# The opening joins the build-time order, and the inverses' triangle is split over two PSUM banks by rows

## The chip, the cores and the metric

The kernel runs on one core of a Trainium2 chip. The metric is device time in microseconds (us) of one execution. Three executions of the kernel before took 611.55, 602.25 and 604.9 us, median 604.9; the profiled execution, from which every row below comes, took 604.67 us.

## The reference

Two stages. The first is a recurrent attention over 4 batches, 8 heads, 768 time steps and a head dimension of 40, with a 40x40 state per batch and head:

```
y[t]  = r[t] . S
Sa    = S . a[t]
S     = S * w[t] - outer(Sa, b[t]) + outer(v[t], k[t])
```

The second treats y, laid out as 3072 tokens of 320 values, as the input of a mixture of 8 experts. A token is computed where x . w_skip > 0; its expert is the argmax of x . w_gate, and the output is x + gate * (relu(x W1) W2), with W1 320x1024 and W2 1024x320. Other tokens pass unchanged.

## The kernel before

**The tiling.** The 768 steps are cut into 24 chunks of 32 steps (c = 0 to 23) and 12 half-phases of 64 (h = 0 to 11); six phases ph hold two half-phases or four chunks each. The 32 pairs of batch and head are spread over partitions and columns, so that one small matmul serves one pair.

**Per half-phase.** The inputs w, k and b, and a are loaded (`load_w`, `load_kb`, `load_a`). VectorE runs two scans (`scan_z`, `scan_w`) that turn the decays into cumulative products, with a clamp and a reciprocal between them (`scan_d`). `kbm` and `l1a` multiply k, b and a by these products, on POOL or VectorE. `wchk` lets ScalarE square w with a running sum, for a range check. `m1` forms the 32x32 products inside a chunk on TensorE; ScalarE copies one half of them into AB, VectorE transposes the other half, which is masked (`fin`) and sent by four DMAs into the left operand L1. `kbt` and `wtt` transpose operands on TensorE.

**Per phase.** The recurrence inside a chunk needs the inverse of a triangular 32x32 matrix for each pair. `tinv` does this on VectorE for phases 1 to 5: a forward substitution with, in each step, a product and a subtraction of the rest of the triangle. The triangle lies in PSUM in two pieces by columns, the first SPL = 12 columns in X0 (32x12 values in each partition) and the other 20 in X1 (20x20). The steps of the two pieces are independent; step i of the loop does step i of X0 and step i+12 of X1, each with a product and a subtraction: 30 products and 30 subtractions for X0, 18 and 18 for X1, 96 in all. ScalarE copies the result to SBUF and a VectorE transpose of 128x1024 puts it in TB. `tinv0` does phase 0 in another way: two 16x16 blocks of the triangle on VectorE in SBUF, the rest by matmuls (`s1`, `s2`, `full`).

**Per chunk.** `ux`, `uq`, `sst` and `yy` are the recurrence, 32 to 64 small matmuls each, for x = 0 and 1. `ux` needs the chunk's R, `uq` multiplies its result by TB, four copies put that into R, a masking on POOL follows, `sst` makes the state for the next chunk's R, `yy` the output Y, which goes out as XS, one DMA per chunk. The router of the experts (`score4`, `route`) runs two chunks behind.

**What sets the order.** Two regimes follow one another. From the first load to the end of chunk 0's pass through the loop, the order is the order of the program's text, written out by hand: the opening. It issues each instruction as it is met (line 117, in `Rec.call`). From c = 1 the recorder is on (`if c==1: rec.on=True`): every call becomes a task with the data that it reads and writes, a cost and a latency, and at c = 22 `flush` orders all tasks of chunks 1 to 21 by a list scheduler at build time (`plan`) and issues them (line 233). The plan starts with every engine free at time 0 and all data from before already there. It knows costs per operation (`cost`), gives each task that uses PSUM a bank, lets VectorE take a ScalarE copy out of PSUM, and counts a DMA as landed a fixed 2.2 us plus its bytes over 170 GB/s after its issue. From c = 22 the text's order holds again (line 117), for the last two chunks and the experts.

**The opening's order.** Half-phases 0 and 1 are loaded and scanned; h = 2 is loaded, and its scans stand ahead of the inverse of phase 0; h = 3 and its scans, `kbm` and `l1a` come between the pieces of `s1` and `s2`. For h = 3 both `kbm` and the first `l1a` are given to VectorE (`kbm(3,1,V); kbm(3,0,V); l1a(3,0,V)`), the second `l1a` to POOL. Chunk 0's second half (`uq(0,1)`) is the first piece of chunk 1's recorded work. Between the steps stand bursts: `zb` and `warm` issue 128x512 matmuls whose result nobody reads (`burst`; BU0 = 6 at the start, the counts of BX after it).

Of the kernel before, what the change touches and what calls it, by code (L numbers as in the profile page):

```python
# [8 lines left out]
F32 = mybir.dt.float32  # L9
# [47 lines left out]
class Rec:  # L57
# [58 lines left out]
    def call(s,e,op,fn,a,k):  # L116
        if not s.on: return fn(*a,**k)  # L117
        def ap(x):
            if x is None or isinstance(x,(int,float,str)): return []
            if hasattr(x,'tensor'): return [x]  # L120
            return ap(x.ap) if hasattr(x,'ap') else []
        w=ap(a[0])+ap(k.get('accum_out'))
        r=[y for x in list(a[1:])+[v for n,v in k.items() if n!='accum_out'] for y in ap(x)]
        W=[u for x in w for u in s.use(x)]; R=[u for x in r for u in s.use(x)]
        d,lat=s.cost(e,op,w,r,a)
        own=dict(s.own)
        L=s.tasks[-1] if s.tasks else None
# [24 lines left out]
    def plan(s,keep=False):  # L152
# [14 lines left out]
        def want(i):  # L167
# [8 lines left out]
                a,k=max(x for x in av if x[0]<=a)  # L176
                got[o]=k; t0=max(t0,a)
            return t0,got
        pos=blk=0; ent=0.0
        done=0; old=sorted(users)  # L180
        while done<N:
            best=None
# [19 lines left out]
            if e=='P':  # L202
                pos+=t.k
                while pos>=256*(blk+1):
                    x=max(fin[i],ent+s.BLK); fin[i]=x; ent=x; blk+=1
            free[e]=fin[i]; [pool[f].remove(i) for f in pool if i in pool[f]]; done+=1; nxt[e]+=1
            for j in t.n:
                rdy[j]=max(rdy[j],fin[i]+t.lat+(s.HOP if e!=T[j].e or t.lat else 0)); left[j]-=1
                if not left[j]: put(j)
            for o in t.al:  # L210
                use.setdefault(o,{})[e]=fin[i]; users[o]-=1; last[o]=max(last.get(o,0),fin[i]+s.HOP)
# [38 lines left out]
class Ring:  # L250
# [4 lines left out]
    def tile(s,shape,dt,tag=None,name=None):  # L255
# [4 lines left out]
        if len(shape)==2: return t  # L260
        ax=["abcd"[q] for q in range(len(shape)-1)]
        return t.rearrange("p ("+" ".join(ax)+") -> p "+" ".join(ax),**{a:v for a,v in zip(ax,shape[1:])})
G2=1; TD=(1,3); BU0=6; BU=(2,0,0,0); BX=(0,0,0,0,0,1,0,0,0,0,2,2,1,1,1,0,0,0,1,2,0,1,1,1,1,0,1,0,0); SPL=12; SCAN_POOL=0; RN=192; RB=((),()); RLAST=(('0c','1b','3a','3c'),('0a','0c')); P2=0
ROUTE=('0c',('0c','1b','3c'),('0c','1b','3c'))
WT=(1,0,0,0,1)
def attn(ctx,tc,i,m,out):
# [174 lines left out]
    def tinv(ph):  # L441
        ab=AB[0]
        NLt=sq(NL_)
        V.transpose(NLt.rearrange("p a b -> p (a b)"),ab.rearrange("p a b -> p (a b)"))
        Xi=sq(X_); K=32-SPL
        X0=ps_x.tile([128,32,SPL],F32); X1=ps_x.tile([128,K,K],F32)
        V.tensor_tensor(X0,NLt[:,0:SPL].rearrange("p s t -> p t s"),m.mT[:,:,0:SPL],ALU.mult)
        V.tensor_tensor(X1,NLt[:,SPL:32,SPL:32].rearrange("p s t -> p t s"),m.mT[:,SPL:32,SPL:32],ALU.mult)
        V.memset(X0.rearrange("p a b -> p (a b)")[:,0:SPL*SPL:SPL+1],-1.0)
        V.memset(X1.rearrange("p a b -> p (a b)")[:,::K+1],-1.0)  # L450
        yield
        for i in range(1,31):
            q=[]
            for g,(j,o,X) in enumerate(((i,0,X0),(i+SPL,SPL,X1))):
                if j>30: continue
                n=31-j; k=min(i,SPL) if g==0 else i
                tv=tmp_[g][:,:n*k].rearrange("p (a b) -> p a b",b=k)
                V.tensor_tensor(tv,NLt[:,j,j+1:32].unsqueeze(2).broadcast_to([128,n,k]),X[:,j-o,0:k].unsqueeze(1).broadcast_to([128,n,k]),ALU.mult)
                q.append((tv,X[:,j+1-o:32-o,0:k]))
            for tv,xv in q: V.tensor_tensor(xv,xv,tv,ALU.subtract)  # L460
            yield
        A.copy(Xi[:,:,0:SPL],X0); A.copy(Xi[:,SPL:32,SPL:32],X1)
# [114 lines left out]
    def yy(c,x):  # L577
# [8 lines left out]
        if x==1:  # L586
# [2 lines left out]
            V.tensor_tensor(xs.rearrange("p (h e) -> p h e",h=8),Y,H[c//2]['WT',cc].rearrange("p h x e -> p (h x) e"),ALU.mult)  # L589
            SP.dma_start(ov[c],xs)  # L590
    def burst(k,l,r):
        pb=ps_s.tile([128,r.shape[1]],F32)
        for _ in range(k): TE.matmul(pb,l,r,start=True,stop=True)
    def warm(k): burst(k,m.tri,m.mc[:,0:512])
    def run_all(g):
        for _ in g: pass
    if 1:

        with tc.manual_schedule(engines={ET.Pool}):
# [9 lines left out]
            G.memset(WR[:,8192:10240],0.0)  # L609
            zero(WR[:,10240:11264])  # L610
            V.memset(l3,0.0)
            load_w(0); load_kb(0); load_a(0); load_w(1,alt[:,0:1041]); load_kb(1); load_a(1,a1)
            m.consts()
            zb=lambda n,q=0: burst(n,zl[:,128*q:128*q+128],z[:,0:512])
            zb(BU0)
            wchk(0,0); wchk(0,1)
# [3 lines left out]
            scan_z(0,None,V); scan_d(0); scan_w(0,V); load_w(2)  # L620
# [6 lines left out]
            ev=[]; late=[]; pq=ps_p; ps_p=Ring.of(ps_p.t+ps_c.t+ps_y.t+ps_x.t)  # L627
            for x in range(2):
                for c in range(2): m1(0,x,c,ev,None,V)
                warm(BX[14+x])  # L630
            for x in range(2):
                for e in ev[2*x:2*x+2]: e()
                l1a(1,x,V)
            load_a(2,L1t[:,3072:4096].rearrange("p (u t) -> p u t",u=16));
            for b in range(4): kbt(0,b); warm(BX[16+b])
            wchk(1,0); wchk(1,1)
            del ev[:]
            scan_z(2,None,V); scan_d(2); scan_w(2,V)
            kbm(2,1); kbm(2,0); l1a(2,0); l1a(2,1)
            for x in range(2):  # L640
                for c in range(2): m1(1,x,c,ev,late)
            for x in range(2): m2(0,x); warm(BX[20+x])
            for e in ev: e()
# [3 lines left out]
            t0=tinv0(Xi); next(t0); tq=[0]  # L647
            def Tb(k,n=0):
                for _ in range(k): next(t0)
                if n: q=tq[0]; tq[0]+=1; V.memset(zl[:,128*q+127:128*q+128],0.0); zb(n,q)  # L650
            ps_p=Ring.of(pq.t+ps_y.t+ps_x.t)
            ux(0,0); wex(0,0); warm(BX[24]); ux(0,1); wtt(0,0); wex(0,1)
            warm(BX[22]); wtt(0,1); warm(BX[23])
            for e in late: e()
            scan_x(1)
            wchk(2,0); wchk(2,1)
            load_w(4); load_kb(4)
            G.memset(L1t[:,2048:3072],0.0)
            ev=[]
            m2(1,0); Tb(4,BX[0]); m2(1,1); Tb(3,BX[1])  # L660
            m1(2,0,0,ev); m1(2,0,1,ev)
            Tb(2,BX[2]); Tb(2,BX[3])
            m1(2,1,0,ev); m1(2,1,1,ev)
            Tb(3,BX[4]); s1,s2,full=next(t0)
            r4=ps_p; ps_p=ps_c
            s1(0,0); warm(BX[5])
            full(0)
            s2(0,0,(0,1,0,1))
            warm(BX[11])
            uq(0,0)  # L670
            for e in ev: e()
            ps_p=r4
            zero(L1t[:,3072:4096])
            scan_z(3,alt[:,1041:2083],V); scan_d(3); scan_w(3,V); kbm(3,1,V); kbm(3,0,V); l1a(3,0,V)
            l1a(3,1); scan_x(2); scan_x(3)
            s1(0,1); warm(BX[6])
            s1(1,0)
            sst(0,0); warm(BX[12])
            s2(0,1,(1,1,1,1))
            s1(1,1); warm(BX[13])  # L680
            load_a(4)
            wchk(3,0); wchk(3,1)
            warm(BX[10])
            ps_p=pq
# [18 lines left out]
            return xl,m.route(xl[:,0:1],1,NC-2,lambda: onehot(0)),onehot  # L703
        for c in range(NC):
            ph,j=divmod(c,4)
            if c==1: rec.on=True
            if c==20: m.load(0)
            if c==22:
                with tc.manual_schedule(engines={ET.Pool}): rec.flush()
# [451 lines left out]
```

## Time and profile before

| | |
|---|---|
| profiled execution | 604.67 us |
| its span, first to last instruction | 602.5 us |
| median of three executions | 604.9 us |
| PE busy | 477.5 us, 79% |
| DVE (VectorE) busy | 463.2 us, 77% |
| ACT (ScalarE) busy | 359.3 us, 60% |
| POOL (GpSimd) busy | 305.3 us, 51% |
| DMA | 82.03 MB, mean 136 GB/s |
| mean granted TensorE clock | 0.908 of full speed |

Busy time counts the overlap of two instructions of an engine once. A line of the profile names a line of the kernel: L117 is whatever was issued in the text's order, L233 whatever the plan ordered. Tiles of the work memory M appear as M whatever their use; px, pc, pq, py and ps are PSUM banks.

### The profile page before, as it was taken

Reading aid. Unit: us, or ns where it says so; the run is one execution under the profiler, and the core shown is the slowest. Engines: PE = TensorE matmul, PEld = TensorE weight load, DVE = VectorE, ACT = ScalarE, POOL = GpSimd, SP = SyncE. Lnnn points to the kernel's source line nnn. Section 1 sums busy time; section 2 is a strip of 40 time slices with the busy share of each in tenths; the row PEclk is TensorE's granted clock in tenths of the full one; section 3 lists DMA queues with packets and bytes.
Section 4 is the critical chain, followed back from the end, with each engine's and each line's share of the span. In section 5 each row is a group of like instructions: output and inputs, shape, how many; then the busy total and the mean of one; then the engine's idle time right before and its main releaser. Section 6 shows DMA issues by size and latency. Waiting matters only on the chain. (4 is left out here: it accounts for less than half of the span.)

```text
span 602.5 us, 28644 instructions
## 1 busy us (share of the span) xinstructions
PE 477.5 (79%) x12452; PEld 397.2 (66%) x12452; DVE 463.2 (77%) x1100; ACT 359.3 (60%) x846; POOL 305.3 (51%) x225
## 2 busy tenths in 40 slices
PE   4784826897878777887798768887478999999995
PEld 1452525776666566666686556665365799999994
DVE  8988948798998699798978879872373558788871
ACT  6462636677768478667666566866265555455530
POOL 5462684465614695257755452403112266666671
PEclk9686968899799899999869979999588999999998
DMA  7874078435452635555543674453652487786100
GB/s 196 216 185 114 20 184 226 106 95 151 112 148 76 156 94 137 132 129 153 124 106 109 165 173 103 112 128 76 167 160 81 126 221 224 226 230 200 41 21 23
DMA packets 80694, 82.03 MB, mean 136 GB/s; under 512 B 49041, under 2 KB 68062, under 8 KB 80099
## 3 DMA queue, kind: packets, MB, share of 16 engines
q1 hardware_dynamic: 78643, 76.35, 48.6%
q0 software_dynamic: 1920, 3.79, 1.8%
q8 instruction: 100, 1.64, 1.2%
q14 instruction: 31, 0.25, 0.1%
HBM read 62.69 MB, written 13.15 MB: 126 GB/s over the span
## 5 line engine op out<-in xcount | busy, mean ns | idle before, releaser
L233 POOL TENSOR_TENSOR R1t<-R1t,mc 64x512 f32<-64x512 f32 x42 | 60.9, 1450 | 90.8 <-ACT R1t L233 51.5
L233 ACT COPY R1t<-pc 32x288 f32<-32x288 f32 (+4 forms) x121 | 52.7, 437 | 20.7 <-PE pc L233 12.5
L117 POOL TENSOR_TENSOR WL<-WR,WH 128x1280 fp32r<-128x1280 f32 (+1 forms) x21 | 58.0, 2798 | 8.4 <-ACT WH L117 8.3
L233 ACT COPY R1t<-px 32x288 f32<-32x288 f32 (+4 forms) x91 | 40.3, 443 | 16.0 <-PE px L233 6.1
L233 POOL TENSOR_TENSOR WR<-WR,M 104x1024 f32<-104x1024 f32 x14 | 32.4, 2334 | 15.1 <-DVE M L233 10.3
L117 ACT CAST WH<-WR 128x1024 fp32r<-128x1024 f32 (+1 forms) x35 | 39.7, 1134 | 0.0
L117 POOL DMA_INDIRECT out<-ro,ti x16 | 15.7, 984 | 45.1 <-DVE ro L117 11.1
L233 DVE TENSOR_TENSOR_SCAN M<-M 104x1041 f32<-104x1041 f32 (+1 forms) x14 | 37.7, 2695 | 0.1
L117 ACT ACTIVATE hH<-pc 128x512 fp32r<-128x512 f32 x21 | 12.6, 599 | 37.9 <-PE pc L117 31.7
L117 DVE TENSOR_TENSOR WL<-WR,WH 128x1024 fp32r<-128x1024 f32 (+1 forms) x19 | 23.8, 1254 | 12.5 <-ACT WH L117 11.9
L117 DVE CAST ti<-xe 128x2 int32<-128x2 f32 x8 | 33.1, 4132 | 0.2
L233 POOL DMA_INDIRECT xg<-XS,ix x18 | 18.4, 1022 | 28.1 <-DVE XS L233 16.8
L117 PE MATMUL pc<-xH,WH 128*128 128x256 f32 x126 | 32.5, 283 | 0.0
L233 POOL TENSOR_TENSOR M<-M,mc 128x256 f32<-128x256 f32 x18 | 18.0, 998 | 26.4 <-DVE M L233 14.8
L233 ACT COPY R1t<-py 32x416 f32<-32x416 f32 (+4 forms) x56 | 25.3, 451 | 8.0 <-PE py L233 4.6
L117 PE MATMUL ps<-WH,hH 128*128 128x320 f32 x88 | 27.6, 314 | 0.0
L117 PE MATMUL pc<-xH,WL 128*128 128x256 f32 x126 | 27.3, 281 | 0.0
L117 PE MATMUL ps<-WL,hH 128*128 128x320 f32 x88 | 27.2, 309 | 0.0
L117 PE MATMUL ps<-WH,hL 128*128 128x320 f32 x88 | 27.2, 309 | 0.0
L233 DVE TENSOR_TENSOR pc<-pc,M 128x48 f32<-128x48 f32 (+20 forms) x96 | 25.8, 269 | 1.8
L117 ACT COPY R1t<-pc 32x416 f32<-32x416 f32 (+3 forms) x36 | 15.6, 440 | 18.0 <-DVE R1t L117 11.6
L117 PE MATMUL ps<-mc 128*128 128x512 f32 x34 | 22.8, 778 | 4.4 <-DMA mc<-mc 2.9
(478 smaller groups left out, 1653.6 us busy)
## 6 DMA issues: line engine op xcount, KB each, us to landing
WR<-w SPq DMA_DIRECT2D x16, 640.0 KB
WR<-w SPq DMA_DIRECT2D x16, 512.0 KB
L2t<-SCR SPq DMA_DIRECT2D x40, 160.0 KB
WR<-kb SPq DMA_DIRECT2D x32, 160.0 KB
WR<-w SPq DMA_DIRECT2D x16, 256.0 KB
R1t<-vt SPq DMA_DIRECT2D x48, 80.0 KB
SV<-vv SPq DMA_DIRECT2D x48, 80.0 KB
out<-XS SPq DMA_DIRECT2D x24, 160.0 KB
```

The costliest lines, as they stand in the source:

```text
L117: if not s.on: return fn(*a,**k)
L233: for fn,a,k,own in s.tasks[i].calls: (fn if s.en[i]==s.tasks[i].e else s.nc.vector.tensor_copy)(*[at(x,own) for x in a],**{n:at(x,own) fo ...
```

## The change

**The order.** `rec.on=True` moves from c = 1 to just before the first load. The opening becomes tasks of the same plan as chunks 1 to 21; memsets ahead of it stay as they are. `burst` returns at once while the recorder is on, so that the bursts of the opening and of chunk 1 are gone; those after the flush (WT, two bursts of two records) remain. The opening's text is rewritten: h = 0 and 1, the inverse of phase 0 with `s1`, `full`, `s2`, then `uq(0,0)`, and only then the loads and scans of h = 2 and 3. `kbm(3,1)`, `kbm(3,0)` and `l1a(3,0)` lose their V and so go to POOL, their default. The plan's data dependencies, not this text, decide what may run when; the text sets the tasks' numbers, which enter their priority.

**The plan's DMA.** A DMA issued by SP now passes through one queue: it begins at the later of the queue's end and its issue plus 1.6 us, adds its bytes over 200 GB/s to the queue's end, and lands 0.4 us later. This holds for every DMA of the plan.

**The inverse.** The triangle is cut by rows: X0 holds rows 0 to 15 (16x16), X1 rows 16 to 31 (16x32). Step j has one product of (31-j) x j values for all rows below, and a subtraction for each bank that has such rows: two for j below 15, one from there on. So 30 products and 44 subtractions, 74 in all, on the same number of values. `tinv0` is unchanged.

```
 class Task:
-    __slots__=(...,"v")
+    __slots__=(...,"v","by")
...
+        t.by=4*int(np.prod([d[1] for d in w[0].ap])) if 'dma' in op else 0
...
-        pos=blk=0; ent=0.0
+        pos=blk=0; ent=dq=0.0
...
+            lat=t.lat
+            if e=='S': dq=max(dq,fin[i]+1.6)+t.by/2e5; lat=dq+0.4-fin[i]
             for j in t.n:
-                rdy[j]=max(rdy[j],fin[i]+t.lat+(s.HOP if e!=T[j].e or t.lat else 0)); left[j]-=1
+                rdy[j]=max(rdy[j],fin[i]+lat+(s.HOP if e!=T[j].e or t.lat else 0)); left[j]-=1
...
-        X0=ps_x.tile([128,32,SPL],F32); X1=ps_x.tile([128,K,K],F32)
+        X0=ps_x.tile([128,16,16],F32); X1=ps_x.tile([128,16,32],F32)
...
-        for i in range(1,31):
-            q=[]
-            for g,(j,o,X) in enumerate(((i,0,X0),(i+SPL,SPL,X1))):
-                if j>30: continue
-                n=31-j; k=min(i,SPL) if g==0 else i
-                tv=tmp_[g][:,:n*k].rearrange("p (a b) -> p a b",b=k)
-                V.tensor_tensor(tv,NLt[:,j,j+1:32].unsqueeze(2).broadcast_to([128,n,k]),X[:,j-o,0:k].unsqueeze(1).broadcast_to([128,n,k]),ALU.mult)
-                q.append((tv,X[:,j+1-o:32-o,0:k]))
-            for tv,xv in q: V.tensor_tensor(xv,xv,tv,ALU.subtract)
+        for j in range(1,31):
+            n=31-j; d=max(0,15-j)
+            tv=tmp_[j%2][:,:n*j].rearrange("p (a b) -> p a b",b=j)
+            V.tensor_tensor(tv,NLt[:,j,j+1:32].unsqueeze(2).broadcast_to([128,n,j]),(X0[:,j] if j<16 else X1[:,j-16])[:,0:j].unsqueeze(1).broadcast_to([128,n,j]),ALU.mult)
+            if d: V.tensor_tensor(X0[:,j+1:16,0:j],X0[:,j+1:16,0:j],tv[:,0:d],ALU.subtract)
+            V.tensor_tensor(X1[:,16-n+d:16,0:j],X1[:,16-n+d:16,0:j],tv[:,d:n],ALU.subtract)
             yield
...
     def burst(k,l,r):
+        if rec.on: return
...
+            rec.on=True
             load_w(0); load_kb(0); load_a(0); load_w(1,alt[:,0:1041]); load_kb(1); load_a(1,a1)
             m.consts()
...
+            t0=tinv0(Xi)
+            for _ in range(15): next(t0)
+            s1,s2,full=next(t0)
+            ux(0,0); wex(0,0); ux(0,1); wtt(0,0); wex(0,1); wtt(0,1)
+            scan_x(1)
+            for w in range(2): s1(0,w)
+            full(0)
+            for w in range(2): s2(0,w,(0,1,0,1))
+            m2(1,0); m2(1,1)
+            uq(0,0)
+            load_w(2); load_a(2,L1t[:,3072:4096].rearrange("p (u t) -> p u t",u=16))
+            scan_z(2,None,V); scan_d(2); scan_w(2,V); wchk(2,0); wchk(2,1); scan_x(2)
+            kbm(2,1); kbm(2,0); l1a(2,0); l1a(2,1)
...
+            scan_z(3,alt[:,1041:2083],V); scan_d(3); scan_w(3,V); wchk(3,0); wchk(3,1); scan_x(3)
+            kbm(3,1); kbm(3,0); l1a(3,0); l1a(3,1)
             load_w(4); load_kb(4)
...
-            if c==1: rec.on=True
```

## Rows read from the trace of the kernel before

**Rows 1.** The view that cuts the span into stretches: for each stretch its length, then each engine's busy us (and instructions), the granted TensorE clock, the DMA engines' busy share and GB/s. The first stretch is the opening, the others the planned chunks up to the end of the last inverse.

```profile
0.00:86.00 86.00, 50.33 (x1186) 29.59 (x1186) 70.51 (x91) 40.81 (x101) 49.39 (x43) 0.80 0.60 150
86.00:143.00 57.00, 46.32 (x1667) 38.64 (x1668) 47.13 (x143) 40.65 (x111) 29.22 (x21) 0.88 0.61 151
143.00:208.00 65.00, 51.62 (x1744) 41.67 (x1742) 59.37 (x165) 45.97 (x116) 33.93 (x25) 0.90 0.48 127
208.00:278.00 70.00, 56.67 (x2110) 46.71 (x2114) 60.32 (x174) 50.19 (x131) 44.88 (x36) 0.97 0.48 125
278.00:343.00 65.00, 53.67 (x1782) 43.77 (x1772) 55.01 (x162) 44.79 (x114) 36.90 (x31) 0.89 0.46 123
343.00:409.00 66.00, 51.84 (x1768) 42.02 (x1769) 54.11 (x185) 45.43 (x116) 21.43 (x21) 0.95 0.53 130
```

**Rows 2.** The timeline at the end of the last inverse: start us, us, engine, line, operation, tiles and shape, count, and in brackets the engine's idle time before it and what ended that.

```profile
406.94 1.94 DVE L233 STREAM_TRANSPOSE TB<-M 128x1024 f32<-128x1024 f32 x1
...
408.94 0.92 PE L233 MATMUL pc<-UX,TB 32*32 32x104 f32 x32 [0.24 <-DVE XS L233]
```

**Rows 3.** The timeline where the text's order hands over to the plan, by engine: ScalarE, SP, TensorE, VectorE.

```profile
84.96 0.72 ACT L233 ACTIVATE junk<-M,wc 104x512 bf16<-104x512 f32 x1 [10.57 <-DMA M<-wt]
...
79.65 0.85 SPq L117 DMA_DIRECT2D M<-wt  x2
...
73.61 0.92 PE L233 MATMUL px<-UX,TB 32*32 32x104 f32 x32
86.54 1.08 PE L233 MATMUL py<-WR,L1t 128*32 128x64 f32 x32 [12.02 <-issue]
...
86.12 0.32 DVE L233 STREAM_TRANSPOSE M<-py 128x128 f32<-128x128 f32 x1 [7.14 <-issue]
```

**Rows 4.** The timeline of VectorE inside the inverse of phase 2 (a subtraction of the first piece, the start of the second piece, then both pieces in turn) and at the tail of that of phase 1, where one piece is left.

```profile
158.87 0.32 DVE L233 TENSOR_TENSOR py<-py,M 128x150 f32<-128x150 f32 x1
159.10 1.43 DVE L233 TENSOR_TENSOR pq<-M,mc 128x400 f32<-128x400 f32 x1
...
160.87 0.32 DVE L233 TENSOR_TENSOR M<-M,py 128x168 f32<-128x168 f32 x1
161.11 0.18 DVE L233 TENSOR_TENSOR M<-M,pq 128x34 f32<-128x34 f32 x1
161.22 0.34 DVE L233 TENSOR_TENSOR py<-py,M 128x168 f32<-128x168 f32 x1
...
135.34 0.17 DVE L233 TENSOR_TENSOR M<-M,px 128x12 f32<-128x12 f32 x1
135.54 0.18 DVE L233 TENSOR_TENSOR px<-px,M 128x12 f32<-128x12 f32 x1
```

**Rows 5.** The timeline of the opening where VectorE and POOL work on SBUF at the same time: a product of VectorE beside one of POOL at 11 to 16 us, a scan alone and a scan beside POOL, and h = 3's `kbm` and first `l1a`. A time that stands for two instructions (x2) is their sum.

```profile
12.45 3.15 DVE L117 TENSOR_TENSOR WR<-M 40x1024 f32<-40x1024 f32 x1
...
11.36 3.17 POOL L117 TENSOR_TENSOR WR<-WR,M 104x1024 f32<-104x1024 f32 x1 [4.92 <-DMA WR<-kb]
...
32.22 2.33 DVE L117 TENSOR_TENSOR_SCAN M<-M 104x1041 f32<-104x1041 f32 x1 [2.37 <-DMA M<-wt]
...
35.08 3.87 DVE L117 TENSOR_TENSOR_SCAN M<-M 104x1040 f32<-104x1040 f32 x1
...
34.62 6.30 POOL L117 TENSOR_TENSOR WR<-WR,M 104x1024 f32<-104x1024 f32 x2 [9.48 <-DVE M L117]
...
65.78 3.89 DVE L117 TENSOR_TENSOR WR<-WR,L2t 104x1024 f32<-104x1024 f32 x2
...
69.59 1.74 DVE L117 TENSOR_TENSOR L1t<-SCR,M 40x1024 f32<-40x1024 f32 x1
```

**Rows 6.** The groups of POOL instructions: busy us, mean ns of one, and idle time before them. And POOL's idle time ahead of chunk 0's masking, from the timeline.

```profile
L233 POOL TENSOR_TENSOR WR<-WR,M 104x1024 f32<-104x1024 f32 x14 | 32.4, 2334 | 15.1 <-DVE M L233 10.3 <-DMA WR<-kb 4.7
L233 POOL TENSOR_TENSOR L1t<-M 40x1024 f32<-40x1024 f32 x8 | 17.5, 2182 | 2.6 <-DVE M L233 2.3
...
65.29 1.63 POOL L117 TENSOR_TENSOR R1t<-R1t,mc 64x512 f32<-64x512 f32 x1 [15.83 <-issue]
```

**Rows 7.** The bursts: one line of the view of the PSUM tile ps for each of the two kinds (count, shortest/median/longest ns of one, first and last start), and the timeline around the burst ahead of `uq(0,0)`.

```profile
L117 PE MATMUL ps<-mc x30: 592/615/1222, 20.5 to 72.1; 128*128 128x512 f32 x30
...
L117 PE MATMUL ps<-SV,SV x12: 592/592/1222, 3.1 to 10.0; 128*128 128x512 f32 x12
...
58.53 3.65 PE L117 MATMUL ps<-mc 128*128 128x512 f32 x4
62.11 0.92 PE L117 MATMUL pc<-UX,TB 32*32 32x104 f32 x32
```

**Rows 8.** The stretches again, ten microseconds each, TensorE alone: busy us (instructions), granted clock, DMA share, GB/s.

```profile
50.00:60.00 10.00, 5.78 (x157) 0.50 0.42 119
...
80.00:90.00 10.00, 3.46 (x118) 0.54 0.82 190
...
100.00:110.00 10.00, 9.84 (x270) 0.51 0.60 159
```

**Rows 9.** ScalarE's last copies of `m1`'s products into AB ahead of the inverse of phase 0 (x2 is the sum of two), and the transpose with which VectorE begins that inverse.

```profile
31.81 0.65 ACT L117 COPY M<-px 128x128 f32<-128x128 f32 x2
...
39.68 1.20 DVE L117 STREAM_TRANSPOSE M<-M 128x1024 f32<-128x1024 f32 x1
```

More of the change, by code (lines that the diff above doesn't have):

```diff
@@ L39 @@
 class Task:
-    __slots__=("e","op","calls","R","W","d","lat","out","p","n","pr","al","up","k","v")
+    __slots__=("e","op","calls","R","W","d","lat","out","p","n","pr","al","up","k","v","by")
 class Eng:
@@ L262, in tile @@
         return t.rearrange("p ("+" ".join(ax)+") -> p "+" ".join(ax),**{a:v for a,v in zip(ax,shape[1:])})
-G2=1; TD=(1,3); BU0=6; BU=(2,0,0,0); BX=(0,0,0,0,0,1,0,0,0,0,2,2,1,1,1,0,0,0,1,2,0,1,1,1,1,0,1,0,0); SPL=12; SCAN_POOL=0; RN=192; RB=((),()); RLAST=(('0c','1b','3a','3c'),('0a','0c')); P2=0
+G2=1; TD=(1,3); BU0=6; BU=(2,0,0,0); BX=(0,0,0,0,0,1,0,0,0,0,2,2,1,1,1,0,0,0,1,2,0,1,1,1,1,0,1,0,0); SCAN_POOL=0; RN=192; RB=((),()); RLAST=(('0c','1b','3a','3c'),('0a','0c')); P2=0
 ROUTE=('0c',('0c','1b','3c'),('0c','1b','3c'))
@@ L444, in tinv @@
         V.transpose(NLt.rearrange("p a b -> p (a b)"),ab.rearrange("p a b -> p (a b)"))
-        Xi=sq(X_); K=32-SPL
-        X0=ps_x.tile([128,32,SPL],F32); X1=ps_x.tile([128,K,K],F32)
[L447 to L450, printed above, removed]
-        yield
-        for i in range(1,31):
-            q=[]
-            for g,(j,o,X) in enumerate(((i,0,X0),(i+SPL,SPL,X1))):
-                if j>30: continue
-                n=31-j; k=min(i,SPL) if g==0 else i
-                tv=tmp_[g][:,:n*k].rearrange("p (a b) -> p a b",b=k)
-                V.tensor_tensor(tv,NLt[:,j,j+1:32].unsqueeze(2).broadcast_to([128,n,k]),X[:,j-o,0:k].unsqueeze(1).broadcast_to([128,n,k]),ALU.mult)
-                q.append((tv,X[:,j+1-o:32-o,0:k]))
-            for tv,xv in q: V.tensor_tensor(xv,xv,tv,ALU.subtract)
+        Xi=sq(X_)
+        X0=ps_x.tile([128,16,16],F32); X1=ps_x.tile([128,16,32],F32)
+        V.tensor_tensor(X0,NLt[:,0:16,0:16].rearrange("p s t -> p t s"),m.mT[:,0:16,0:16],ALU.mult)
+        V.tensor_tensor(X1,NLt[:,:,16:32].rearrange("p s t -> p t s"),m.mT[:,16:32],ALU.mult)
+        V.memset(X0.rearrange("p a b -> p (a b)")[:,::17],-1.0)
+        V.memset(X1.rearrange("p a b -> p (a b)")[:,16::33],-1.0)
+        yield
+        for j in range(1,31):
[4 more added lines that the diff above has]
+            V.tensor_tensor(X1[:,16-n+d:16,0:j],X1[:,16-n+d:16,0:j],tv[:,d:n],ALU.subtract)
             yield
-        A.copy(Xi[:,:,0:SPL],X0); A.copy(Xi[:,SPL:32,SPL:32],X1)
+        A.copy(Xi[:,0:16,0:16],X0); A.copy(Xi[:,16:32],X1)
         s0=(2*ph)%NTB; s1=(2*ph+1)%NTB
@@ L611, in attn @@
             V.memset(l3,0.0)
+            rec.on=True
             load_w(0); load_kb(0); load_a(0); load_w(1,alt[:,0:1041]); load_kb(1); load_a(1,a1)
             m.consts()
-            zb=lambda n,q=0: burst(n,zl[:,128*q:128*q+128],z[:,0:512])
-            zb(BU0)
-            wchk(0,0); wchk(0,1)
             for x in range(2): zero(fR(x,0))
@@ L619, in attn @@
             load_vv(0,0); load_vv(0,1); load_rr(0); load_kb(2)
-            scan_z(0,None,V); scan_d(0); scan_w(0,V); load_w(2)
+            scan_z(0,None,V); scan_d(0); scan_w(0,V)
+            wchk(0,0); wchk(0,1)
             kbm(0,1); kbm(0,0,V); l1a(0,0,V); scan_z(1,alt[:,1041:2083],V); l1a(0,1,V)
@@ L626, in attn @@
             zero(Xi.rearrange("p a b -> p (a b)"))
-            ev=[]; late=[]; pq=ps_p; ps_p=Ring.of(ps_p.t+ps_c.t+ps_y.t+ps_x.t)
             for x in range(2):
-                for c in range(2): m1(0,x,c,ev,None,V)
-                warm(BX[14+x])
+                for c in range(2): m1(0,x,c,FE=V)
+                l1a(1,x,V)
+            for b in range(4): kbt(0,b)
+            wchk(1,0); wchk(1,1)
             for x in range(2):
-                for e in ev[2*x:2*x+2]: e()
-                l1a(1,x,V)
@@ L634, in attn @@
[L634 to L643, printed above, removed]
+                for c in range(2): m1(1,x,c)
@@ L644, in attn @@
+            for x in range(2): m2(0,x)
             for x in range(2):
                 for c in range(2): SP.dma_start(L2[x][0][64*x:64*x+64,c],i['idl'][x,64*x:64*x+64])
-            load_kb(3); load_w(3,alt[:,0:1041]); load_a(3,a1)
[L647 to L656, printed above, removed]
-            load_w(4); load_kb(4)
[L658 to L680, printed above, removed]
+            t0=tinv0(Xi)
@@ L681, in attn @@
+            kbm(2,1); kbm(2,0); l1a(2,0); l1a(2,1)
+            load_kb(3); load_w(3,alt[:,0:1041]); load_a(3,a1)
+            for w in range(2): s1(1,w)
+            G.memset(L1t[:,2048:3072],0.0)
+            m1(2,0,0); m1(2,0,1); m1(2,1,0); m1(2,1,1)
+            zero(L1t[:,3072:4096])
+            scan_z(3,alt[:,1041:2083],V); scan_d(3); scan_w(3,V); wchk(3,0); wchk(3,1); scan_x(3)
+            kbm(3,1); kbm(3,0); l1a(3,0); l1a(3,1)
+            load_w(4); load_kb(4)
+            sst(0,0)
             load_a(4)
-            wchk(3,0); wchk(3,1)
@@ L683, in attn @@
-            warm(BX[10])
-            ps_p=pq
             for x in range(2):
```

## The prediction

> **What bounds the kernel now.** I read the stretches first, to see which engine sets the pace in each part, then the end of the last inverse, then the place where the two orders meet, and last the single instructions that the change touches. In the first 409 us VectorE is busy 346.5 us, the sum of its six entries, or 85%; TensorE is busy 310.5 us, 76%, ScalarE and POOL less [rows 1]. That VectorE's queue ends this part, and not the recurrence, is seen at its end: the transpose that finishes the last inverse runs from 406.94 to 408.88 us, and the matmul that needs it starts 0.06 us later [rows 2]. What follows takes the remaining 193.6 us of the span and is untouched by the change, so I take a microsecond of VectorE's queue saved before 408.9 us as a microsecond of the total, as long as nothing else becomes late.
>
> VectorE's idle time before that point is 62.6 us. 25.4 us of it lie in the first 143 us (15.5 and 9.9), the other 37.2 in the four stretches after [rows 1]. The largest single piece stands where the text's order hands over to the plan: ScalarE waits 10.57 us for a load of w that SP issued only at 79.65 us, behind it wait the copies that empty m1's bank, TensorE is idle 12.02 us and VectorE 7.14 us [rows 3]. The plan, starting with all earlier data "there", had put the range check on that load first.
>
> **The change part by part.** *The seam.* With one plan from the first load on there is no place where data under way counts as landed, and the copies need not stand behind the check. On VectorE's queue the stall is worth 7.1 us; the ends are 0 (it forms again elsewhere) and 12.0, TensorE's idle time [rows 3]. I take -7.1, since VectorE is the engine whose sum matters. If it goes, what is late next is the first full inverse, which needs h = 2 and 3 scanned.
>
> *The inverse.* Per inverse 22 of 96 instructions go, 110 in all; the values, 2 x 4960, stay. The price hangs on whether neighbours depend on each other. Independent neighbours: 168 values start 0.24 us before the next, 34 values 0.11 us, so 0.97 ns per value and 0.08 us fixed. Dependent ones: 0.20 us for 12 values, so 0.19 us fixed [rows 4]. Before, with the pieces in turn, 18 double steps cost 4 x 0.08 and 12 single ones 2 x 0.19: 10.4 us fixed. After, 14 steps cost 0.19 + 0.08 + 0.08 (the second subtraction covers the first) and 16 cost 2 x 0.19: 11.0 us. So perfect alternation before would make the change cost 0.6 us per inverse, 3 in all; if every removed instruction gave back the dependent price, it would save 4.2 per inverse, 21 in all. Between +3 and -21 I take -5, near the first end, because rows 4 show neighbours overlapping, a little below it because the plan knows nothing of that overlap and does not alternate strictly; the piece that starts late (159.10 us, after the first has done six steps) shows it [rows 4].
>
> The Trainium skill, page "VectorE: DVE Perf Modes", section "The DRAIN you can't avoid", says that the next instruction does not start until the pipe is empty, and advises to lower the count of instructions. By it the sum would take -21 here, that is 571 us; the trace disagrees, with 0.11 us between two starts where the first runs 0.18 [rows 4].
>
> *The three products that move.* kbm(3,1), kbm(3,0) and l1a(3,0) leave VectorE, 3.89 + 1.74 = 5.6 us [rows 5], for POOL, at 2 x 2.33 + 2.18 = 6.9 us [rows 6]. POOL has room, idle 15.8 us around there before [rows 6]; queued behind the three are the maskings of chunk 0 and of m1(2), which yy and L1's DMAs wait for. But POOL's products slow VectorE's: a product of 40x1024 takes 3.15 us and ends 1.1 us after POOL's, a scan takes 3.87 us beside POOL against 2.33 alone [rows 5]. If each of the three hits a neighbour for 1.5 us, 1.0 of the 5.6 is left; if none, all of it. I take -3.
>
> The Trainium skill, page "SBUF — State Buffer", section "SBUF: two separate sides", speaks against this move: a VectorE instruction with two SBUF inputs and a POOL instruction that reads SBUF exclude each other for the whole instruction. By it the move could give back up to POOL's 6.9 us and cost 1.3 on balance, 591 us in all; the 3.15 us row agrees, but the loop's steps read one operand from PSUM.
>
> *The rest of the opening's order.* The 2.37 us that VectorE waits for w(2) [rows 5] goes, as other work is there by then: -2.4, the ends 0 and -2.4. The inverse of phase 0 could start when AB is complete, at 32.46 us and not at 39.68 [rows 9]; but the scans that stand there are done later on the same queue, so 0 for the sum. On SP the loads of w(2) and a(2) pass behind four idl DMAs and L1's; DMA engines are busy 60% in the opening [rows 1], and VectorE's queue of half-phases 0 and 1 covers it. If the cover is gone, the scan of h = 2 waits again, for about those 2.4 us. POOL's later kbm(2) follows the scan as before. PSUM banks are given by the plan now; I cost that at 0, covered by TensorE's 46 idle us in the first 143.
>
> *The bursts.* 30 + 12 records go, about 18.5 + 7.1 = 26 us of TensorE at their medians; one group of 3.65 us stood directly ahead of uq(0,0) [rows 7]. TensorE doesn't bound here: 0, with a gain of 3.7 at most; the loss is a rival below.
>
> *The plan's DMA queue* alters the order of all chunks up to 21. No row shows the new order. I take 0, and as bounds a quarter of VectorE's 37.2 idle us there: -9 to +9.
>
> Sum: -7.1 - 5 - 3 - 2.4 = -17.5. The profiled execution's own time is 604.67 us, 2.2 more than its span and 0.2 below the median of the three runs, so no correction is needed: **587 us**.
>
> **The rivals.** *The stall only moves* (597 us, 592 to 605). SP issues in order, ScalarE too; a check planned on a load that lands later than counted blocks the copies again, somewhere in the first 100 us where DMA is 60% busy. Then the seam and the 2.4 us are not gained, and 604.7 - 5 - 3 = 597 remains. For it: 10.57 us show what one such miss costs [rows 3]. Against: the queue is now counted.
>
> *TensorE at its lower clock* (622 us, slower). Without bursts the clock may stand at 1.2 GHz, half of full speed, through the opening. TensorE's work of the first 143 us without bursts is 96.7 - 26 = 71 us at a mean of 0.83; at 0.5 it takes 118, 47 more. VectorE's 25.4 idle us can cover that much of it, 22 are left, and only the inverse's 5 are gained: 604.7 + 22 - 5 = 622. It decides when the granted clock is near 0.5 through most of that time; at 0.7 the addition is 13 us and covered. For it: even with bursts the clock fell to 0.50 at 50 to 60 us and to 0.54 where TensorE had stood still [rows 3, 8]. Against: the stretches from 143 us on have no bursts and stand at 0.89 to 0.97 [rows 1].
>
> *The opening packs fully* (576 us, 567 to 578). All of VectorE's 25.4 idle us but 5 for the first load go, 20.4 and not 9.5: 604.7 - 20.4 - 5 - 3 = 576; with the -9 above, 567. For it: all operands of later phases may now fill gaps. Against: maskings, copies and matmuls take the same time as before.
>
> *Each removed instruction gives back its full dependent price* (571 us), as worked out above.
>
> **How the numbers follow.** Forecast 0.51 (own range 578 to 597), moved stall 0.21, lower clock 0.09, packed opening 0.11, full price 0.08. The range, 570 to 604, leaves out the slow case, the lowest part of the packed one and the edge of the moved stall. About 2%, 12 us, is what a measurement of this kernel can tell from no change: faster is below 592.8, slower above 617. Three quarters of the forecast, 0.38, with 0.11 and 0.08 make 0.57 faster; 0.13 and 0.21 make 0.34 within; 0.09 slower.
>
> **What would show it.** Nearly all lines before the flush are L233; ps<-mc of 128x512 is down to 4 records, ps<-SV gone. No engine idles 10 us on a load of w. An inverse has 74 steps' instructions on VectorE, and a subtraction that follows its product starts about 0.2 us behind it. The three products stand on POOL. The last TB<-M transpose ends near 391 us, with the same 194 us after it. The forecast is wrong if VectorE's idle time up to there is not below 55 us, if its busy time has grown through POOL, if the clock in the first 143 us is below 0.65, or if the last transpose comes early and the time after it has grown.

## The result, and the profile after

Four executions of the changed kernel took 584.29, 577.68, 580.74 and 587.8 us, median 582.51, beside 603.58 for the kernel before (four executions). The ratio is 0.9639, with a 95% interval of 0.9584 to 0.9694: faster, by 21.8 us of 604.9. Ratios, here and below, leave out executions in a slower state (here 587.8 and 611.55). The forecast was 587 us in a range of 570 to 604, faster by 17.5 us. The profiled execution is the one of 584.29 us (span 582.5), 20.4 us below that of before. Lines that the plan orders are L236 now.

Busy time, share of the span and instructions of each engine, from the page of the changed kernel:

```profile
PE 454.0 (78%) x12408; PEld 393.5 (68%) x12408; DVE 458.4 (79%) x1006; ACT 355.2 (61%) x827; POOL 309.9 (53%) x228
```

The stretches of the changed kernel, with the columns of [rows 1]:

```profile
0.00:86.00 86.00, 35.49 (x1242) 30.96 (x1243) 69.19 (x99) 45.69 (x114) 50.48 (x41) 0.74 0.66 171
86.00:143.00 57.00, 44.93 (x1684) 38.08 (x1687) 50.57 (x125) 34.69 (x88) 34.43 (x27) 0.82 0.51 126
143.00:208.00 65.00, 52.13 (x1859) 42.66 (x1847) 58.79 (x149) 47.32 (x119) 36.42 (x29) 0.92 0.50 130
208.00:278.00 70.00, 56.79 (x2035) 47.45 (x2035) 62.37 (x158) 53.49 (x136) 50.81 (x40) 0.93 0.48 124
278.00:343.00 65.00, 51.96 (x1903) 42.45 (x1905) 52.98 (x153) 46.23 (x118) 35.39 (x32) 0.95 0.48 126
343.00:409.00 66.00, 55.98 (x1979) 45.62 (x1967) 51.06 (x156) 47.85 (x118) 19.49 (x17) 0.97 0.48 120
```

VectorE is about as busy in each stretch as before [rows 1]: 345.0 us up to 409, where it was 346.5. What differs is how far the work has come by then. That is seen better when the cuts are the same events in both kernels, the ends of the first and of the last full inverse. The kernel before:

```profile
0.00:139.50 139.50, 94.83 (x2769) 66.64 (x2769) 116.58 (x232) 80.25 (x205) 78.62 (x64) 0.83 0.60 150
139.50:408.90 269.40, 215.57 (x7463) 175.70 (x7463) 229.86 (x687) 187.61 (x478) 137.14 (x110) 0.93 0.49 127
```

And the changed kernel:

```profile
0.00:141.40 141.40, 78.82 (x2874) 67.65 (x2878) 118.19 (x221) 78.94 (x198) 83.57 (x67) 0.77 0.60 153
141.40:382.60 241.20, 196.15 (x7030) 161.43 (x7023) 210.54 (x572) 175.96 (x445) 136.35 (x111) 0.93 0.49 127
```

The first full inverse ends no earlier: at 141.4 us instead of 139.5. The first matmul that needs it, chunk 4's, does start 3.4 us earlier, the kernel before first:

```profile
145.99 0.92 PE L233 MATMUL py<-UX,TB 32*32 32x104 f32 x32
...
142.58 0.92 PE L236 MATMUL pc<-UX,TB 32*32 32x104 f32 x32
```

Before, it stood 6.5 us behind the end of its transpose, now 1.2. The four inverses after it take 241.2 us instead of 269.4, 28.2 less. Up to the last one VectorE's busy time fell from 346.4 to 328.7 us (-17.7) and its idle time from 62.5 to 53.9 (-8.6): 26.3 us together. Of these, 6.3 do not reach the end: 199.9 us follow the last inverse, where 193.6 did before. Nor has all of the 17.7 us gone: over the whole span VectorE's busy time fell by 4.8 us (463.2 to 458.4), and behind the last inverse it rose from 116.8 to 129.6, as the plan now puts work there that stood ahead of it.

The timeline at the end of the last inverse, which answers to [rows 2]:

```profile
380.58 2.00 DVE L236 STREAM_TRANSPOSE TB<-M 128x1024 f32<-128x1024 f32 x1
...
386.29 0.51 ACT L236 COPY UX<-py 128x416 f32<-128x416 f32 x1
...
388.51 0.92 PE L236 MATMUL pc<-UX,TB 32*32 32x104 f32 x32
```

The matmul that needs the transpose now starts 5.9 us after its end, not 0.06: its other operand, UX, was copied only from 386.29 to 386.80 us (before, by 405.46, ahead of the transpose's end), and behind it TensorE still had other products in its order. The chunks' own chain came last there, VectorE's inverse no longer. Counted from this matmul, the end is as far off as before: 194.0 us, where it was 193.6.

In the opening, the waits of the first 143 us (what was waited for, total us, times, longest). VectorE and ScalarE:

```profile
DVE M L236 <- ACT M L236: 6.2, 4, 4.5
DVE SCR L236 <- ACT M L236: 3.2, 2, 1.9
DVE R1t L236 <- PE py L236: 2.9, 1, 2.9
...
ACT L2t L236 <- DVE M L236: 9.1, 1, 9.1
ACT XS L236 <- DMA mc<-mc: 8.3, 1, 8.3
```

No engine waits 10 us on a load of w any more [rows 3]; VectorE's waits are on other engines' results instead. The timelines of TensorE and VectorE show what came later and what did not, chunk 0's `uq` and the start of the first full inverse:

```profile
73.44 1.61 PE L236 MATMUL ps<-UX,TB 32*32 32x104 f32 x32 [8.80 <-DVE TB L236]
...
89.46 1.20 DVE L236 STREAM_TRANSPOSE M<-M 128x1024 f32<-128x1024 f32 x1
```

In the kernel before, that inverse starts 0.4 us later:

```profile
89.87 1.20 DVE L233 STREAM_TRANSPOSE M<-M 128x1024 f32<-128x1024 f32 x1
```

`uq(0,0)` stands 11.3 us later than before [rows 7]. VectorE began the inverse of phase 0 earlier, at 34.96 us and not at 39.68 [rows 9], but by its timeline four scans of h = 2 and 3 stand among its steps and behind them, from 46.87 to 71.02 us, ahead of the copies that complete TB.

### The profile page after: what moved, and what is told of

Read it like the earlier page. It is cut to its first block, busy times and chain, and to the rows that moved or that the text cites. A ratio compares the mean times of both kernels' runs of the same rounds, so it can differ in the third digit from the quotient of the medians.

```text
span 582.5 us, 28434 instructions
## 1 busy us (share of the span) xinstructions
PE 454.0 (78%) x12408; PEld 393.5 (68%) x12408; DVE 458.4 (79%) x1006; ACT 355.2 (61%) x827; POOL 309.9 (53%) x228
## 5 line engine op out<-in xcount | busy, mean ns | idle before, releaser
L236 POOL TENSOR_TENSOR R1t<-R1t,mc 64x512 f32<-64x512 f32 x43 | 62.7, 1458 | 97.4 <-ACT R1t L236 59.9
L236 POOL TENSOR_TENSOR WR<-WR,M 104x1024 f32<-104x1024 f32 x19 | 43.7, 2310 | 24.9 <-DVE M L236 18.7
L236 ACT COPY R1t<-pc 32x288 f32<-32x288 f32 (+5 forms) x105 | 44.8, 428 | 11.8 <-PE pc L236 5.0
L236 DVE TENSOR_TENSOR_SCAN M<-M 104x1041 f32<-104x1041 f32 (+1 forms) x20 | 49.5, 2475 | 0.2
L236 ACT COPY R1t<-px 32x288 f32<-32x288 f32 (+4 forms) x73 | 32.6, 448 | 20.7 <-PE px L236 9.1
L117 POOL DMA_INDIRECT out<-ro,ti x16 | 15.7, 981 | 44.0 <-DVE ro L117 10.5
L236 ACT COPY R1t<-py 32x416 f32<-32x416 f32 (+5 forms) x67 | 29.8, 444 | 10.0 <-PE py L236 4.8
L117 DVE CAST ti<-xe 128x2 int32<-128x2 f32 x8 | 35.2, 4397 | 0.2
L236 DVE TENSOR_TENSOR px<-px,M 128x16 f32<-128x16 f32 (+21 forms) x104 | 31.1, 299 | 1.7
L236 POOL DMA_INDIRECT xg<-XS,ix x18 | 18.4, 1022 | 18.9 <-DVE pq L236 3.4
L236 ACT COPY R1t<-pq 32x288 f32<-32x288 f32 (+4 forms) x53 | 23.0, 433 | 6.9 <-PE pq L236 2.5
L236 POOL TENSOR_TENSOR M<-M,mc 128x256 f32<-128x256 f32 x20 | 20.4, 1020 | 12.5 <-DVE M L236 8.1
L117 PEld LDWEIGHTS pc<-xH,WH 128*128 128x128 f32 x126 | 23.8, 189 | 0.0
```

The lines of the kernel that those rows point to most:

```text
L236: for fn,a,k,own in s.tasks[i].calls: (fn if s.en[i]==s.tasks[i].e else s.nc.vector.tensor_copy)(*[at(x,own) for x in a],**{n:at(x,own) fo ...
```

## The experiments

All were timed in five rounds beside the kernel before. Its median was 609.17 us in the first group (the first four below), 605.13 in the second (the next four) and 604.56 in the third, so only ratios are compared; "x us" is a ratio's distance from 1, or from another ratio, times 604.7.

**The inverse alone** (the kernel before, with only the part of the diff that cuts the triangle by rows).

> The kernel before with the inverse by rows alone; the opening, the plan's costs and its DMA as before. Theory (VectorE's queue sets the pace, and a removed instruction gives back about 0.1 us): each inverse occupies VectorE some 2.3 us less, 11 us over five, so about 593 us, ratio to before 0.980 to 0.988. Rival 1 (neighbours overlap, so the removed ones were nearly free): ratio 0.993 to 1.005. Rival 2 (what the change gains comes from the order of the opening alone): ratio 1.0.

Ratio 0.9768 (0.9734 to 0.9802), -14.0 us. In its trace, by tile, the transposes that end an inverse (count, ns of one, first and last start):

```profile
L233 DVE STREAM_TRANSPOSE TB<-M x5: 1947/2010/2031, 133.0 to 392.8; 128x1024 f32<-128x1024 f32 x5
```

The last one starts 14.1 us earlier than in [rows 2]. The inverse was worth nearly three times my term, and more than the theory's range. But in this kernel the inverse does not come last: the first matmul of phases 1 to 5 starts 12.1, 14.9, 14.6, 5.0 and 5.1 us behind the end of its transpose. How VectorE's time reached the chunks here is not shown.

**The order alone** (the changed kernel with the inverse cut by columns again).

> The changed kernel with the old inverse by columns; the opening in the plan and the plan's DMA queue stay. Theory: the 11 us of the inverses are missing, so 0.975 to 0.985 of before. Rival 1 (the inverse is free): as the changed kernel, 0.964. Rival 2 (the order of the opening gives nothing): 1.0.

Ratio 0.9844 (0.9808 to 0.9880), -9.4 us. The two halves multiply to 0.9768 x 0.9844 = 0.9616, inside the interval of the whole. That ratios multiply is not shown, though: a pair further below misses its product, so that the match may be chance.

**The three products back on VectorE** (in the changed kernel).

```
-            kbm(3,1); kbm(3,0); l1a(3,0); l1a(3,1)
+            kbm(3,1,V); kbm(3,0,V); l1a(3,0,V); l1a(3,1)
```

> The changed kernel with h = 3's two kbm and first l1a back on VectorE. Theory: 5.6 us return to VectorE's queue, of which about half was given back by POOL's blocking, so +1 to +4 us, ratio to before 0.965 to 0.971. Rival (POOL's products block VectorE for as long as they run): 0 to -2 us, 0.960 to 0.964.

Ratio 0.9794 (0.9753 to 0.9835), 9.4 us more than the whole change and more than either theory gave. But the plan makes another order from this input all the way to chunk 21, and the last experiments show what that alone can be worth; so this run doesn't price the move.

**The plan without the DMA queue** (in the changed kernel; two PSUM banks are zeroed at the start by ScalarE).

```
-            if e=='S': dq=max(dq,fin[i]+1.6)+t.by/2e5; lat=dq+0.4-fin[i]
+            if e=='S': dq=max(dq,fin[i]+1.6)+t.by/2e5; lat=t.lat
```

> The changed kernel with the plan's old DMA latency (2.2 us plus bytes over 170 GB/s from the issue, no queue). Two PSUM banks are zeroed by ScalarE at the start, 1 us before the first load lands. Theory (the queue model keeps ScalarE and VectorE from standing behind loads that come late): waits of several us on DMA loads are back in the first 140 us, 0.970 to 0.985 of before. Rival (the opening's gain does not depend on it): 0.960 to 0.968, and no wait over 3 us on a load.

Ratio 0.9919 (0.9884 to 0.9953), 17 us more than the whole change and above the theory's range. Its timeline of TensorE's first matmuls, and of VectorE's first work on them:

```profile
27.28 1.52 PE L236 MATMUL py<-rrt,SV 40*32 40x64 f32 x31 [27.28 <-DMA SV<-vv]
...
37.31 1.08 PE L236 MATMUL py<-WR 128*32 128x64 f32 x32
...
38.53 0.32 DVE L236 STREAM_TRANSPOSE M<-py 128x128 f32<-128x128 f32 x1 [12.29 <-PE py L236]
```

In the changed kernel TensorE begins with that product of WR:

```profile
21.24 1.08 PE L236 MATMUL py<-WR 128*32 128x64 f32 x32 [21.24 <-DVE WR L236]
```

Counted as landed 2.2 us after their issue, the loads of v put their product first in TensorE's order; it stands there until 27.28 us, and the first product that VectorE waits for comes 16 us late. The lateness lies mostly in the issue: by SP's timeline the four loads of v go out from 7.32 to 22.83 us, one behind the other, and in the changed kernel as slowly (7.75 to 22.48); there another product stands first. A load of w also holds ScalarE for 5.1 us again. This is my rival of the moved stall, and the queue is what keeps it out.

**The hand-over one chunk earlier** (in the kernel before).

```
-            if c==1: rec.on=True
+            if c==0: rec.on=True
```

> The kernel before with the recorder on from c = 0, one stage earlier, so that chunk 0's pass (load of w for h = 5 among it) is planned with its latency; opening text, bursts, inverse and DMA costs as before. Theory (the stall where the orders meet is worth what VectorE and ScalarE lose in it): the 10 us ScalarE wait on w and VectorE's 7 us are gone, ratio to before 0.983 to 0.990. Rival (the stall only moves, or VectorE's work would have waited anyway): 0.995 to 1.005, with another wait of several us within the next 60 us.

Ratio 0.9937 (0.9894 to 0.9980), -3.8 us, between the theories. Its waits from 60 to 143 us:

```profile
ACT junk L233 <- DMA M<-wt: 1.3, 2, 1.0
...
ACT UX L233 <- PE pc L233: 5.1, 1, 5.1
...
PE pc L233 <- DMA R1t<-vt: 4.4, 1, 4.4
```

The wait on w has gone from 10.57 to 1.3 us, and a load of v, which this plan also counts as landed early, holds TensorE for 4.4 and ScalarE behind it for 5.1. About half of the stall moved.

**The DMA queue alone** (in the kernel before, all lines of the diff on `by`, `dq` and `lat`).

> The kernel before with the plan's DMA queue alone. Theory (it matters only where many loads stand close, in the opening, which is not planned here): the hand-over keeps its stall of about 10 us, ratio 0.992 to 1.005. Rival (the queue is what makes the planned order better everywhere): 0.975 to 0.985.

Ratio 1.0078 (1.0040 to 1.0117), +4.7 us, outside both ranges. ScalarE's wait at the hand-over stays:

```profile
ACT junk L236 <- DMA M<-wt: 10.1, 1, 10.1
```

The load was issued before the plan begins, where no queue in the plan can see it. Without the opening in it, the queue gains nothing and costs a little.

**Another order of each kernel** (HOP, the plan's price of a step between engines).

```
-    HOP=0.08; PW=1.25; BLK=3.6
+    HOP=0.09; PW=1.25; BLK=3.6
```

> The changed kernel with the plan's hand-over cost between engines 0.09 us for 0.08: same work, another order. Theory (the gain lies in the parts of the change, not in one lucky order): 0.955 to 0.975 of before. Rival (the order is a lucky draw): 0.975 to 0.99.

> The kernel before with the plan's hand-over cost 0.09 us for 0.08: same work, another order. It shows what an order is worth by itself. Theory: 0.99 to 1.01. Rival (the order of the kernel before is a poor draw): 0.975 to 0.985.

The changed kernel gave 0.972 (0.9658 to 0.9782), the kernel before 1.002 (0.9979 to 1.0061).

**No bursts in the opening** (in the kernel before; BU0 and the opening's counts of BX are 0, two records in chunk 1 stay; two PSUM banks are zeroed at the start by ScalarE).

> The kernel before without the opening's bursts (42 records); the plan of chunks 1 to 21, its one burst included, is the same, and ScalarE zeroes two PSUM banks in a gap at the start. Theory (the bursts cost and give nothing that the end sees): ratio 0.994 to 1.005. Rival 1 (without them TensorE works at its lower clock and the opening grows): 1.008 to 1.03, the granted clock of the first 86 us well below 0.74. Rival 2 (they stand in the way of chunk 0): 0.985 to 0.993.

Ratio 0.9904 (0.9863 to 0.9945), -5.8 us. The first stretch, with the columns of [rows 1], and from the timelines `uq(0,0)` and the start of the first full inverse:

```profile
0.00:86.00 86.00, 35.10 (x1240) 30.19 (x1240) 73.22 (x94) 45.09 (x111) 52.88 (x44) 0.74 0.62 159
...
57.66 2.31 PE L117 MATMUL pc<-UX,TB 32*32 32x104 f32 x31 [0.75 <-DVE TB L117]
...
86.52 1.20 DVE L233 STREAM_TRANSPOSE M<-M 128x1024 f32<-128x1024 f32 x1
```

The granted clock of the stretch falls from 0.80 to 0.74, and yet `uq(0,0)` comes 4.4 us earlier than in [rows 7]. So the bursts stood in the way. Where the 5.8 us sit further on, its trace doesn't tell: the profiled execution took 604.85 us, and its last inverse ended no earlier than before.

**The three products on POOL, alone** (in the kernel before; its plan is the same).

```
-            ...scan_w(3,V); kbm(3,1,V); kbm(3,0,V); l1a(3,0,V)
+            ...scan_w(3,V); kbm(3,1); kbm(3,0); l1a(3,0)
```

> The kernel before with h = 3's two kbm and first l1a on POOL; the plan of chunks 1 to 21 is the same. Theory (5.6 us leave VectorE, about half comes back through POOL's blocking): 0.993 to 0.998. Rival (POOL's products block VectorE for all of their 6.9 us, or the maskings behind them are late): 1.000 to 1.006.

Ratio 1.0033 (0.9991 to 1.0074): nothing is saved. VectorE's timeline at the hand-over:

```profile
86.91 0.32 DVE L233 STREAM_TRANSPOSE M<-py 128x128 f32<-128x128 f32 x1 [12.89 <-ACT M L233]
```

VectorE waits 12.89 us here, where it waited 7.14 [rows 3], and starts no earlier: the 5.6 us became 5.75 us of waiting ahead of the same moment.

**A third order of the changed kernel** (LET, another constant of the plan, from 1.0 to 0.9).

> The changed kernel with the plan's allowance for letting an earlier task in front at 0.9 us for 1.0: same work, another order, to see with after_hop9 how far one order lies from the next. Theory: 0.96 to 0.98 of before, within 1% of the changed kernel's 0.964. Rival (the changed kernel's order is an outlier): 0.98 or more.

Ratio 0.963 (0.958 to 0.968). With 0.9639 and 0.972, the changed kernel's orders spread over 0.9%, while the two orders of before differ by 0.2%. No order tried is faster than the changed kernel's by more than the interval.

**The inverse and the earlier hand-over together** (in the kernel before).

> The kernel before with the inverse by rows and the recorder on from c = 0: the two parts that were measured alone (0.977 and 0.994). Theory (they add): 0.966 to 0.976, so that the planned opening and its DMA queue add under 1% to them. Rival (the planned opening is what counts): 0.976 to 0.985.

Ratio 0.9847 (0.9802 to 0.9893): worse than the inverse alone, outside the range that adding the two gave, and at the upper end of the rival's. TensorE waits for the same load of v as above, and the last inverse ends early:

```profile
PE pc L233 <- DMA R1t<-vt: 6.7, 1, 6.7
...
L233 DVE STREAM_TRANSPOSE TB<-M x5: 1990/1999/2032, 136.2 to 387.9; 128x1024 f32<-128x1024 f32 x5
```

The transpose starts 19.0 us earlier than in [rows 2], more than with the inverse alone, but 204.9 us follow it instead of 193.6: the matmul that needs it starts only 8.6 us behind its end. What VectorE gained was not what came last there. Why the whole is slower than the inverse alone, its trace does not tell.

The last transpose's start, the time from its end to the end of the span, the start of the first matmul that needs it (chunk 20's), and the time from there to the end of the span, one profiled execution each; executions of one kernel differ by several us, so small differences between the lines show little:

| kernel | ratio | last transpose, us | after it, us | its matmul, us | from there, us |
|---|---|---|---|---|---|
| before | 1 | 406.9 | 193.6 | 408.9 | 193.6 |
| changed | 0.9639 | 380.6 | 199.9 | 388.5 | 194.0 |
| inverse alone | 0.9768 | 392.8 | 200.8 | 400.0 | 195.7 |
| order alone | 0.9844 | 395.0 | 197.3 | 399.2 | 195.1 |
| earlier hand-over | 0.9937 | 400.4 | 200.4 | 406.8 | 196.0 |
| both of these: inverse, hand-over | 0.9847 | 387.9 | 204.9 | 398.6 | 196.3 |
| products on POOL, alone | 1.0033 | 404.6 | 196.9 | 406.7 | 196.8 |
| DMA queue alone | 1.0078 | 408.4 | 195.3 | 410.4 | 195.2 |

## Why the prediction was right, and where not

**What bounds.** Right for the point that the prediction read, and only in part for the rest. In the kernel before, the first matmul of phases 4 and 5 starts 0.06 us or less behind the transpose that it needs, but in phases 1 to 3 it starts 6.5, 10.6 and 1.8 us behind it: there something else came last. In the changed kernel, from phase 1 to 5, it is 1.2, 0.06, 0.48, 0.15 and 5.9 us. Of the 26.3 us that VectorE gained up to the last transpose 20.4 reached chunk 20's matmul and the profiled time. "The same 194 us after it" failed by 6.3 us as written, counted from the transpose, and holds from the matmul on: 194.0 us, and 193.6 to 196.8 over the table. So a microsecond of VectorE was a microsecond of the total only "as long as nothing else becomes late", and the chunks' own chain became late. My own sign for this ("the last transpose comes early and the time after it has grown") came true in part.

**The inverse, -5: the right mechanism, mis-sized; -14.0 alone.** From the start times of all of VectorE's instructions, an inverse takes 22.2 us before and 20.0 after: five times 2.2 are 11 us; for the other 3 I have no shown cause, and the one profiled execution (597.5 us, 7.2 below that of before) doesn't hold all of the 14. The prices that I had taken held. Over the five inverses, dependent neighbours have a fixed price of 0.195 us before and 0.196 after, independent ones 0.08 in both, against my 0.19 and 0.08. What failed is the count, above all the step "before, with the pieces in turn". I had 24 dependent pairs per inverse before and 46 after; the traces have 192 / 5 = 38 and 178 / 5 = 36. Independent neighbours fell from about 180 to 95 over the five. The plan did not alternate the two pieces strictly. In the kernel before, VectorE's timeline while the piece pc still had steps to do:

```profile
123.52 0.31 DVE L233 TENSOR_TENSOR M<-M,px 128x156 f32<-128x156 f32 x1
123.86 0.33 DVE L233 TENSOR_TENSOR px<-px,M 128x156 f32<-128x156 f32 x1
124.23 0.30 DVE L233 TENSOR_TENSOR M<-M,px 128x144 f32<-128x144 f32 x1
124.57 0.32 DVE L233 TENSOR_TENSOR px<-px,M 128x144 f32<-128x144 f32 x1
...
125.24 0.30 DVE L233 TENSOR_TENSOR px<-px,M 128x132 f32<-128x132 f32 x1
125.45 0.19 DVE L233 TENSOR_TENSOR M<-M,pc 128x48 f32<-128x48 f32 x1
```

Instructions that depend on the one before, of 144 and 156 values, start 0.34 to 0.37 us before the next; only where px changes to pc is it 0.21. In the changed kernel the order inside a step helps without any care of the plan:

```profile
96.46 0.17 DVE L236 TENSOR_TENSOR pq<-pq,M 128x16 f32<-128x16 f32 x1
96.58 0.19 DVE L236 TENSOR_TENSOR px<-px,M 128x26 f32<-128x26 f32 x1
96.68 0.19 DVE L236 TENSOR_TENSOR pq<-pq,M 128x32 f32<-128x32 f32 x1
96.81 0.24 DVE L236 TENSOR_TENSOR M<-M,px 128x84 f32<-128x84 f32 x1
97.08 0.20 DVE L236 TENSOR_TENSOR px<-px,M 128x36 f32<-128x36 f32 x1
97.19 0.20 DVE L236 TENSOR_TENSOR pq<-pq,M 128x48 f32<-128x48 f32 x1
97.32 0.27 DVE L236 TENSOR_TENSOR M<-M,px 128x108 f32<-128x108 f32 x1
```

Subtractions of px and pq start 0.10 to 0.11 us apart, and the next product needs only the bank px, so that it too may follow the pq subtraction at once, 0.13 us behind its start; the one dependent pair shown is from product to subtraction, 96.81 to 97.08. My sign "about 0.2 us" was right for the small steps; here 84 values take 0.27. The rival of the full price, -21 or 571 us, was not reached, but -14.0 is nearer to its -21 than to my -5.

The Trainium skill, page "VectorE: DVE Perf Modes", section "The DRAIN you can't avoid", says that the next operation does not start until the pipe is empty, and goes on to say that one which is not held starts earlier. 0.12 us between two starts where the first runs 0.17 agrees with that second half, which the prediction left out.

**The seam, -7.1: mis-sized; -3.8 alone.** The wait on w goes, but the step "if it goes, what is late next" named the scans of h = 2 and 3, and next came a load of v. In the full change neither load holds an engine; without the plan's queue a load of w and the loads of v do.

**The three products, -3: not shown.** Alone they gave nothing, +2.0 us with an interval from -0.5 to 4.5. POOL's blocking was my reason for less than 5.6; the run shows another one, a wait that ends at the same moment. In the changed kernel VectorE's own `kbm` and `l1a` take 5.8 us less (6.7 where they took 12.5), and POOL's blocking does appear there, beside the two `kbm` of h = 3:

```profile
64.22 4.62 POOL L236 TENSOR_TENSOR WR<-WR,L2t 104x1024 f32<-104x1024 f32 x2 [3.05 <-DVE L2t L236]
...
64.56 2.26 DVE L236 COPY TB<-M 128x512 f32<-128x512 f32 x1
...
66.74 4.28 DVE L236 TENSOR_TENSOR_SCAN M<-L2t,M 104x1040 f32<-104x1040 f32 x1
```

Without POOL beside them such a copy took 0.60 us and such a scan 2.33, so 3.6 of the 5.8 us go back, near the half that I took. Whether the rest reaches the end stays open.

**The opening's order, -2.4: wrong.** The wait for w(2) is gone, but VectorE's idle time in the first 143 us fell only from 25.4 to 23.2 us, where this term and the seam had it fall by 9.5; the other 6.5 us of idle time went in the planned chunks behind. More work stands ahead of the first full inverse on VectorE: 23 copies out of PSUM, 7.7 us, instead of 12, 4.4 us, and the steps of phase 0's inverse occupy it 12.9 us instead of 10.4, as three of them take 1.9 to 2.2 us each beside products of POOL, where before one did. That chunk 4 starts 3.4 us earlier all the same shows that the inverse was not what came last there before. "The opening packs fully" did not come.

**The bursts, 0 with a gain of 3.7 at most: too small; -5.8 alone.** The rival of the lower clock took them to be needed. Its mechanism did appear: TensorE alone, ten microseconds each, as [rows 8], in the changed kernel:

```profile
40.00:50.00 10.00, 3.31 (x50) 0.50 0.65 179
50.00:60.00 10.00, 4.05 (x87) 0.50 0.45 115
60.00:70.00 10.00, 3.14 (x256) 0.50 0.67 194
70.00:80.00 10.00, 5.18 (x252) 0.50 0.38 112
```

The clock stood at 0.50, the 1.2 GHz level, for 40 us, but TensorE had only 15.7 us of work in them. Half speed there cost at most half of that, and over the first 141.4 us the mean stayed at 0.77. The rival's error is that it stretched all of the opening's work.

**The DMA queue, 0 within 9: inside the bounds,** but it is no term by itself. Alone it costs 0.8%; without it the planned opening loses 2.8% (0.9919 against 0.9639). It is a condition of the rest.

**The sum.** -14.0 for the inverse and -9.4 for the order, where I had -5 and -12.5: two errors of opposite sign, so that 587 was near in part by luck. The range held 582.51.

**Still open.** 0.9937 x 0.9904 = 0.984 equals the order's 0.9844, as if hand-over and bursts were all of it; but the two were not run together, and the inverse with the earlier hand-over shows that ratios need not multiply. What of the order's half is a good draw among orders, at a spread of 0.9%, isn't settled either.

## What to carry to other kernels

Judge an earlier result by the instruction that needs it: of VectorE's 26.3 us 5.9 were a wait there for the chunk's other work. Count dependent neighbours in the trace, instruction by instruction, before pricing a change of their number; an order that the code seems to suggest is not the one that a scheduler has made. Time saved ahead of a wait on something else is worth nothing until that wait moves, so look at the next wait on the same queue first. When a scheduler is given more to plan, tell it first when loads land: an in-order engine planned on an early landing stands still with all that is behind it.

## What the runs showed of the hardware that was not expected

TensorE at half its clock for 40 us, with 39% of that time busy, in a kernel that is 3.6% faster; and 42 records of bursts in the opening whose removal alone gave 0.9904. A step of 28 values on VectorE took 2.20 us beside a product of POOL, and 0.19 without one. In the plan without the queue SP took from 7.32 to 22.83 us to issue four loads of v, where the plan counts 0.6 us for each, and their product waited until 27.28 us. And from the first matmul that needs the last inverse, the rest, about a third of the kernel, took 193.6 to 196.8 us in all kernels of the table, while counted from the transposes it ran from 193.6 to 204.9.
